# Fourier mixing and gated convolution FFN: a held load, earlier tables, unread products, and a one-row product in the first chunk

## Chip, cores, metric

One core of one Trainium2 chip. The metric is device time of one execution in microseconds (us), median over runs; the span that a trace shows is about 2 us shorter than the time of the same run. Engines: PE multiplies matrices (TensorE), DVE is VectorE, ACT is ScalarE, POOL is GpSimd, and SP's queue (SPq) issues most loads. The granted clock is the share of full speed at which PE was let run; half clock is 0.5.

## The reference, cut

```python
X = np.fft.fft(x, axis=1)                 # x: 8 x 3136 x 256
X = np.fft.fft(X, axis=2).real            # then the FFN on it:
h = np.maximum(X @ w_in, 0.0)             # 256 -> 1024
conv_out[s] = sum(conv_w[k] * h[s + k - 1] for k in range(3))
out = (h * sigmoid(conv_out)) @ w_out     # 1024 -> 256
```

The kernel folds x by the symmetries of the transform, multiplies it with tables along the sequence, and multiplies the transform over D into w_in beforehand (G). Steps run over (batch, chunk of the sequence, block f of 128 features): 8 x 4 x 8 = 256 steps. The feature D/2 has no partner under the symmetry. It adds to each step a product of a row over the sequence (`er`) and a column over the features (`ge`). Each half of a batch's x comes by one plain load and four gathers (indirect loads that POOL issues). The tables along the sequence are loaded in part, and ACT completes them by copies with either sign; I call that mirroring. The products with them come in odd units first, then even units.

## The kernel before: the parts concerned

```python
w_in[0].load(nc.sync); w_cv.load(nc.scalar)
nc.scalar.dma_start(out=dm, in_=dft_dim[:, :, 0:2])      # dm: table over D
for h in range(2):
    for f in load_ops(0, h, nc.sync, nc.scalar): f()     # x of batch 0, two halves
...
for g in range(2):                                       # sets the "written" bits of pa's two banks
    mm(psa.tile(...), dm[:, 0, g, :], dm.rearrange("p t g i -> p (t g i)"), True, True)
narrow_in(0); blocks(0)                                  # w_in from 64-bit words; G of quarter 0
ops = fold_ops(0)
for f in ops[0:4]: f()
nc.gpsimd.tensor_copy(tabs[1][0:1, 0, 0, 0:1], xh[0, 1][0:1, 0, 0, 0:1])   # releases the tables
for par in (1, 0): load_tables(par)
for i in (1, 2, 3): w_in[i].load(nc.sync)
for f in ops[4:]: f()
w_out.load(nc.sync)
# odd units (DFT), row(): er <- qt by DMA
narrow_in(1)                                             # DVE, while PE makes the even units
# feature, even units; after the feature: flip(), store(), spread(0, all chunks): er -> DRAM -> eb
...
def seed(s):                                             # ACT writes the D/2 part into pa
    act(pa[s][:, 0:n], eb[b, c], AF.Copy, scale=ge[:, f:f + 1])
def products(s):                                         # PE; pb: one product, pa: two or one
    mm(pb[s][:, 0:n], G[0:P-1, 1, fs], PQ[b][1][...], True, True)
    mm(pa[s][:, 0:n], G[:, 0, fs], PQ[b][0][...], False, not triple(s))
# cycle t: products(t+1), copies(t+1) [ACT], combine(t) [DVE], narrowings [DVE],
#          seed(t+2), first_tap(t) [ACT], other_taps(t-1) [DVE], gate(t-2) [DVE, POOL],
#          mm2(t-3) [PE], blocks [PE]
# narrow(2) in cycles 0, 1; narrow(3) in 2, 3; w_out's eight parts in 1 to 8; blocks(1) before cycle 0
```

A narrowing turns a half quarter of w_in (or an eighth of w_out) from 64-bit words into fp32: seven DVE operations, 2.58 us. `blocks(i)` multiplies quarter i with dm into G and `ge`. I call the DVE operation that joins pa and pb of step t combine(t); combine(0) is the first DVE operation of the steps.

Of the kernel before, what the change touches and what calls it, by code (L numbers as in the profile page):

```python
# [9 lines left out]
F32 = mybir.dt.float32  # L10
I32 = mybir.dt.int32
U32 = mybir.dt.uint32
AF = mybir.ActivationFunctionType
# [23 lines left out]
def kernel(  # L37
# [10 lines left out]
    nc = tc.nc  # L48
    B, S, D = x.shape
    F = moe_w_in.shape[1]  # L50
    P = 128
# [16 lines left out]
    xp = ctx.enter_context(tc.tile_pool(name="xp", bufs=2))  # L68
# [11 lines left out]
    psa = ctx.enter_context(tc.tile_pool(name="psa", bufs=2, space=PSUM))  # L80
    psb = ctx.enter_context(tc.tile_pool(name="psb", bufs=1, space=PSUM))
# [6 lines left out]
    act = nc.scalar.activation  # L88

    def mm(o, l, r, start, stop):  # L90
        nc.tensor.matmul(o, l, r, start=start, stop=stop, skip_group_check=True)  # L91

    def spare():

        return pso.tile([P, 2, D], F32, name="po", tag="po").rearrange("p a d -> p (a d)")
# [4 lines left out]
    xh, wt, ea = {}, {}, {}  # L100
# [4 lines left out]
    nc.gpsimd.memset(sg[:, 0], -1.0)  # L105
    nc.gpsimd.memset(sg[:, 1], 1.0)

    def load_ops(b, h, eng, other=None):


        def plain():
            t = xp.tile([P, 8, 2, D], F32, name="xh", tag="xh")
            xh[b, h] = t
            eng.dma_start(out=t[0:NP, 0:4], in_=bass.AP(
                tensor=x.tensor, offset=x.offset + (b * S + 1 + 2 * h) * D,
                ap=[[HQ * D, NP], [Q4 * D, 4], [1, 2 * D]]))

        def zero():
            t = xh[b, h]
            for s0, n, r in ((0, 4, 0), (4, 3, 1), (7, 1, 0)):  # L120
                (other or eng).dma_start(out=t[NP:KR, s0:s0 + n], in_=bass.AP(
                    tensor=x.tensor, offset=x.offset + (b * S + r * Q4) * D,
                    ap=[[D, 1], [Q4 * D, n], [0, 2], [1, D]]))

        def mirrored(m):
            def f():
                nc.gpsimd.indirect_dma_start(  # L127
                    out=xh[b, h][0:NP, 7 - m].rearrange("p q d -> p (q d)"),
                    out_offset=None,
                    in_=bass.AP(tensor=x.tensor, offset=x.offset,  # L130
                                ap=[[2 * D, B * S // 2], [1, 2 * D]]),
                    in_offset=bass.IndirectOffsetOnAxis(ap=idx[0:NP, 0:1], axis=0),
                    element_offset=(b * S + (4 - m) * Q4 - HO + 2 * (1 - h)) * D)
            return f
        return [plain] + [zero] * h + [mirrored(m) for m in range(4)]
# [59 lines left out]
    tabs = [const.tile([P, n, HQ, HE], F32, name="tab%d" % n) for n in (2, 4)]  # L195
    PQ, eb, er = {}, {}, {}
# [5 lines left out]
    def load_tables(par):  # L202


        st = slice(2 * par, 2 * par + 2)
        to = tabs[par][:, 0:2].rearrange("p s q i -> p s (q i)")
        n = HQ * HE
        m = NP // 2 // 16 * 16
        for i in range(2):
            nc.sync.dma_start(out=to[i:2 * m:2], in_=dft_seq[0:m, st, HQ * i:HQ * (i + 1)]  # L210
                              .rearrange("p s q i -> p s (q i)"))
        assert NP == 2 * m + 2
        nc.sync.dma_start(out=to[2 * m:NP], in_=bass.AP(
            tensor=dft_seq.tensor, offset=dft_seq.offset + (m * 4 + 2 * par) * NQ * HE,
            ap=[[n, 2], [NQ * HE, 2], [1, n]]))
        nc.sync.dma_start(out=to[NP:KR], in_=bass.AP(
            tensor=dft_seq.tensor, offset=dft_seq.offset + ((NP * 4 + 2 * par) * NQ - HQ + 2) * HE,
            ap=[[n, 1], [NQ * HE, 2], [1, n]]))
# [141 lines left out]
    def spread(b, cs):  # L360

        for c in cs:
            ch = chunks[c]
            eb[b, c] = ebp.tile([P, HN], F32, name="eb", tag="eb")[:, 0:ch.k1 - ch.k0]
            nc.sync.dma_start(out=eb[b, c], in_=ed[b:b + 1, ch.k0:ch.k1].to_broadcast([P, ch.k1 - ch.k0]))
# [31 lines left out]
    chunks = [Chunk(c) for c in range(len(CUTS))]  # L397
    HW = max(c.w for c in chunks)
    HN = max(c.k1 - c.k0 for c in chunks)
    left = const.tile([P, NF, P], F32, name="left")  # L400
# [52 lines left out]
    dm = gp.tile([P, 2, 2, P], F32, name="dm", tag="g")  # L453
    N4 = F // 4
# [3 lines left out]
    def raw_in(i):  # L458
        def f(sh):
# [5 lines left out]
    w_in = [Weight(w4[i], moe_w_in[:, i * N4:(i + 1) * N4].rearrange("(t p) n -> p t n", p=P), raw_in(i))  # L465
            for i in range(4)]
    w_in[0].load(nc.sync)
    w_cv.load(nc.scalar)
    nc.scalar.dma_start(out=dm, in_=dft_dim[:, :, 0:2])
    for h in range(2):  # L470
        for f in load_ops(0, h, nc.sync, nc.scalar):
            f()
    wout = const.tile([P, NF, D], F32, name="wout")
    G = const.tile([P, 2, F], F32, name="G")
    ge = const.tile([P, NF], F32, name="ge")
    cw = const.tile([P, 3, NF], F32, name="cw")

    def blocks(i):


        w = w4[i]
        for g in range(2):
            p = spare()
            for t in range(2):
                mm(p[:, 0:N4], dm[:, t, g, :], w[:, t], t == 0, t == 1)
            nc.scalar.copy(out=G[:, g, i * N4:(i + 1) * N4], in_=p[:, 0:N4])
        p = spare()
        for m in range(NF // 4):
            for t in range(2):
                mm(p[:, m:m + 1], w[:, t, m * P:(m + 1) * P], dm[:, t, 1, P - 1:P], t == 0, t == 1)  # L490
        nc.scalar.copy(out=ge[:, i * NF // 4:(i + 1) * NF // 4], in_=p[:, 0:NF // 4])

    def taps():
        p = spare()
        mm(p[:, 0:3 * NF], cw24[:, 0], ident, True, True)
        nc.scalar.copy(out=cw.rearrange("p k m -> p (k m)"), in_=p[:, 0:3 * NF])
# [2 lines left out]
    rows = out.rearrange("b s d -> (b s) d")  # L499
    hs, gs, pa, pb, po, nb = {}, {}, {}, {}, {}, {}  # L500

    def cut(s):
        b, c, f = s
        ch = chunks[c]
        return ch, ch.k1 - ch.k0, slice(f * P, (f + 1) * P)

    def seed(s):

        b, c, f = s
        ch, n, fs = cut(s)  # L510
        pa[s] = psa.tile([P, 512], F32, name="pa", tag="pa")
        act(pa[s][:, 0:n], eb[b, c], AF.Copy, scale=ge[:, f:f + 1])  # L512

    def triple(s):

        return s[0] == 0 and s[1] * NF + s[2] < TRIPLE
# [7 lines left out]
    def products(s):  # L524
        b, c, f = s
        ch, n, fs = cut(s)
        pb[s] = psb.tile([P, 512], F32, name="pb", tag="pb")
        mm(pb[s][:, 0:n], G[0:P - 1, 1, fs], PQ[b][1][0:P - 1, ch.k0:ch.k1], True, True)
        mm(pa[s][:, 0:n], G[:, 0, fs], PQ[b][0][:, ch.k0:ch.k1], False, not triple(s))
        if triple(s):  # L530
            mm(pa[s][:, 0:n], G[0:P - 1, 1, fs], PQ[b][1][0:P - 1, ch.k0:ch.k1], False, True)

# [80 lines left out]
    def narrow_in(i):  # L613
        for t in range(2):
            w_in[i].narrow(t, slice(0, N4))

    w_cv.narrow(0, slice(0, P))
    taps()

    for g in range(2):  # L620
        mm(psa.tile([P, 512], F32, name="pa", tag="pa"), dm[:, 0, g, :], dm.rearrange("p t g i -> p (t g i)"),
           True, True)
    narrow_in(0)
    blocks(0)
    ops = fold_ops(0)
    for f in ops[0:4]:
        f()

    nc.gpsimd.tensor_copy(tabs[1][0:1, 0, 0, 0:1], xh[0, 1][0:1, 0, 0, 0:1])
    for par in (1, 0):  # L630
        load_tables(par)
    for i in (1, 2, 3):
        w_in[i].load(nc.sync)
    for f in ops[4:]:
        f()
    w_out = Weight(wout, moe_w_out.rearrange("(c p) o -> p c o", p=P),
                   lambda sh: xp.tile(sh, I32, name="raw", tag="xh"))
    w_out.load(nc.sync)
    begin, us, row, flip, store = units(0)
    begin()  # L640

# [8 lines left out]
    for i, u in enumerate(odds):  # L650
# [2 lines left out]
        u.fin()  # L653
        if i == 1:
            row()
    narrow_in(1)
    mend_row(0, half)
    for i, u in enumerate(us[j] for j in (4, 2, 3, 7, 8)):
        u.matmuls(0, 1)
        u.copy()  # L660
        u.fin()
        if i == 0:
            flip()
            store()
            spread(0, range(len(chunks)))
            for f in load_ops(1, 0, nc.sync):
                f()

    steps = [(b, c, f) for b in range(B) for c in range(len(chunks)) for f in range(NF)]
    per = len(chunks) * NF  # L670
    side = {}

    def at(cycle, where, fn):
        side.setdefault((cycle, where), []).append(fn)

    for i in (2, 3):
        for t in range(2):
            at(2 * i - 4 + t, "dve", lambda i=i, t=t: w_in[i].narrow(t, slice(0, N4)))
        at(2 * i - 3, "pe", lambda i=i: blocks(i))
    for c in range(NF):  # L680
        at(1 + c, "dve", lambda c=c: w_out.narrow(c, slice(0, D)))
    for j, fn in enumerate(load_ops(1, 1, nc.sync)):
# [10 lines left out]
    for b in range(1, B):  # L693
        ops = fold_ops(b)
        c0, n = fold_at[b]
# [10 lines left out]
        c0, n = dft_at[b]  # L706
# [18 lines left out]
    n = len(steps)  # L725
# [1 line left out]
    seed(steps[1])  # L727
    products(steps[0])
    copies(steps[0])
    blocks(1)  # L730
    for t in range(n + LAG):
        def run(where):
            for fn in side.get((t, where), []):
# [88 lines left out]
```

## Time and profile before

| | kernel before |
|---|---|
| time, median of 3 runs | 1265.25 us (1264.12 to 1265.77) |
| span of the profiled execution | 1265.2 us |
| PE / DVE / ACT / POOL busy | 94 / 91 / 70 / 31 % |
| tables issued / first mirrored by ACT | 20.80 / 30.24 us |
| combine(0) / combine(5) | 58.79 / 95.72 us |

A timeline line reads: start, duration, engine, line of the kernel, operation, out<-in, shapes, count, and in brackets the engine's idle time before it with what ended it. A window line reads: window, its length, busy us of PE, PE weight load, DVE, ACT, POOL (with counts), granted PE clock as a share of full, DMA share, GB/s.

### The profile page before, as it was taken

The page shows a single profiled execution, that of the slowest core. Times are in us where ns is not written, and L with a number is a line of the kernel's source. Part 1 is how long each engine was busy: PE and PEld are TensorE (multiplying, and loading weights), DVE is VectorE, ACT ScalarE, POOL GpSimd, SP SyncE. Part 2 cuts the span into 40 slices and gives each one's busy share as a digit, 9 for nine tenths or more (in the row PEclk, how much of TensorE's full clock was granted, in tenths as well). Part 3 has the DMA queues.
Part 4 walks back from the last instruction along what each step waited for, and adds up shares of the span by engine and source line. Part 5 has one row for each costly group of instructions (what it writes and reads, how often), then busy time and mean ns, then how long its engine had stood idle before and what let it go on. Part 6 is the DMA issues. An engine that isn't in the chain of part 4 may idle for free.

```text
span 1265.2 us, 15611 instructions
## 1 busy us (share of the span) xinstructions
PE 1190.4 (94%) x4898; PEld 896.7 (71%) x4898; DVE 1148.7 (91%) x1753; ACT 886.5 (70%) x1847; POOL 396.3 (31%) x501
## 2 busy tenths in 40 slices
PE   2877999899999999999999999999999999999998
PEld 1545677677677767677677777777777777777776
DVE  7499999999999989899899988998999878899996
ACT  1354666677767767777767777776777778788885
POOL 4202642424333234242423324242322213222222
PEclk8799999999999999999999999999999999999999
DMA  7601321212212003020202103120011001010000
GB/s 196 204 1 32 96 77 45 58 34 69 68 53 69 29 19 93 25 84 25 73 23 64 49 26 90 31 84 1 26 45 33 30 26 39 27 28 30 30 25 31
DMA packets 47762, 66.06 MB, mean 52 GB/s; under 512 B 5756, under 2 KB 35348, under 8 KB 47680
## 3 DMA queue, kind: packets, MB, share of 16 engines
q1 hardware_dynamic: 42227, 51.91, 13.4%
q0 software_dynamic: 5120, 12.85, 3.6%
q8 instruction: 39, 0.64, 0.2%
q10 hardware_dynamic: 333, 0.30, 0.1%
q14 instruction: 43, 0.35, 0.1%
HBM read 39.26 MB, written 25.74 MB: 51 GB/s over the span
## 4 chain that ended last, share of the span: by engine, by line
PE 62%; DVE 23%; issue 6%; ACT 4%; DMA 3%; POOL 1%; SPq 0%; DVEq 0%; POOLq 0%; ACTq 0%
PE po L91 38%; PE pb L91 9%; PE pa L91 8%; DVE g L567 7%; PE pd L91 6%; DVE h L555 3%; DVE g L588 3%; ACT nb L544 2%; DVE xh L152 1%; DVE xh L163 1%; DVE w L179 1%; ACT g L580 1%; DMA eb<-ed 1%; DMA er<-qt 1%; DVE w L180 1%
## 5 line engine op out<-in xcount | busy, mean ns | idle before, releaser
L91 PE MATMUL po<-wout,g 128*128 128x256 f32 x3072 | 715.1, 382 | 37.2 <-DVE g L588 33.2
L91 PEld LDWEIGHTS po<-wout,g 128*128 128x128 f32 x3072 | 578.6, 190 | 198.9 <-DVE g L588 76.6
L567 DVE SCALAR_TENSOR_TENSOR g<-h,cw,g 128x770 f32<-128x770 f32 (+1 forms) x512 | 554.0, 1082 | 10.6 <-ACT g L561 1.5
L587 POOL TENSOR_TENSOR g<-g,h 128x385 f32<-128x385 f32 (+1 forms) x256 | 238.5, 932 | 738.7 <-ACT g L580 525.2
L580 ACT ACTIVATE g<-g 128x385 f32<-128x385 f32 (+2 forms) x512 | 244.4, 528 | 224.5 <-DVE g L567 224.2
L544 ACT ACTIVATE nb<-pb 128x386 f32<-128x386 f32 (+2 forms) x484 | 213.3, 494 | 83.8 <-PE pb L91 82.9
L555 DVE CUSTOM_DVE_ANT_0 h<-pa,nb 128x386 f32<-128x386 f32 (+2 forms) x498 | 258.2, 558 | 9.9 <-ACT h L541 9.1
L561 ACT ACTIVATE g<-h,cw 128x770 f32<-128x770 f32 (+1 forms) x256 | 243.6, 951 | 0.2 <-DVE h L555 0.2
L91 PE MATMUL pb<-qt,G 127*128 127x387 f32 (+2 forms) x512 | 215.2, 501 | 3.5 <-DVE qt L277 1.8
L91 PE MATMUL pa<-pt,G 128*128 128x387 f32 (+2 forms) x512 | 212.9, 496 | 3.3 <-ACT pa L512 3.3
L512 ACT ACTIVATE pa<-eb,ge 128x387 f32<-128x387 f32 (+2 forms) x256 | 154.0, 602 | 5.2 <-DMA eb<-ed 5.2
L588 DVE TENSOR_TENSOR g<-g,h 128x385 f32<-128x385 f32 (+1 forms) x256 | 151.7, 593 | 1.3 <-ACT g L580 1.3
L91 PEld LDWEIGHTS pa<-pt,G 128*128 128x128 f32 x512 | 96.8, 190 | 78.4 <-issue 19.0
L91 PE MATMUL pd<-tab,w 98*128 98x196 f32 (+3 forms) x448 | 117.4, 374 | 0.0
L91 PEld LDWEIGHTS pb<-qt,G 127*128 127x128 f32 x512 | 94.3, 191 | 26.1 <-issue 5.6
L127 POOL DMA_INDIRECT xh<-in_x_dram,idx x64 | 96.6, 1509 | 18.1 <-issue 12.9
L91 PEld LDWEIGHTS pd<-tab,w 98*128 98x128 f32 (+1 forms) x448 | 82.9, 190 | 12.8
L607 ACT COPY os<-po 128x256 f32<-128x256 f32 x196 | 58.0, 396 | 10.3 <-PE po L91 5.9
L152 DVE TENSOR_TENSOR xh<-xh 98x1020 f32<-98x1020 f32 (+1 forms) x32 | 45.3, 1419 | 3.6 <-DMA xh<-in_x_dram,idx 3.6
L163 DVE TENSOR_TENSOR xh<-xh 98x1024 f32<-98x1024 f32 (+1 forms) x32 | 40.5, 1266 | 0.1
L181 POOL COPY w<-xh 98x4 f32<-98x4 f32 (+1 forms) x32 | 24.5, 765 | 19.6 <-DVE xh L163 14.5
L339 POOL TENSOR_TENSOR er<-as 1x197 f32<-1x197 f32 (+1 forms) x16 | 13.0, 812 | 55.8 <-ACT as L331 29.3
(94 smaller groups left out, 406.3 us busy)
## 6 DMA issues: line engine op xcount, KB each, us to landing
out_dram<-os SPq DMA_DIRECT2D x192, 128.0 KB
xh<-in_x_dram SPq DMA_DIRECT2D x16, 784.0 KB
eb<-ed SPq DMA_DIRECT2D x16, 193.5 KB
tab<-dft_seq_dram SPq DMA_DIRECT2D x4, 589.5 KB
raw<-in_moe_w_in_dram SPq DMA_DIRECT2D x4, 512.0 KB
raw<-in_moe_w_out_dram SPq DMA_DIRECT2D x1, 2048.0 KB
eb<-ed SPq DMA_DIRECT2D x8, 209.0 KB
eb<-ed SPq DMA_DIRECT2D x8, 193.0 KB
```

The source lines that it names most:

```text
L91: nc.tensor.matmul(o, l, r, start=start, stop=stop, skip_group_check=True)
L127: nc.gpsimd.indirect_dma_start(out=xh[b, h][0:NP, 7 - m].rearrange("p q d -> p (q d)"), out_offset=None, in_=bass.AP(tensor=x.tensor, offs ...
L152: vt(a[:, :, :, 1:D], a[:, :, :, 1:D], r[:, :, :, D - 1:0:-1], op=ALU.add)
L512: act(pa[s][:, 0:n], eb[b, c], AF.Copy, scale=ge[:, f:f + 1])
L544: act(nb[s][:, i, cols], p[:, cols], AF.Copy, scale=-1.0 if i else 1.0)
L555: nc.vector._custom_dve(TENSOR_ADD_SAT, out=to, in0=a[:, cols], in1=c[:, i, cols], s0=BIG, s1=0.0)
L561: act(gs[s], hs[s][:, 0:n], AF.Copy, scale=cw[:, 0, s[2]:s[2] + 1])
L567: stt(out=g, in0=h[:, k:k + n], scalar=cw[:, k, f:f + 1], in1=g, op0=ALU.mult, op1=ALU.add)
L580: act(gs[s][:, c], gs[s][:, c], AF.Sigmoid)
L587: gt(g[:, p], g[:, p], h[:, p], op=ALU.mult)
L588: vt(g[:, v], g[:, v], h[:, v], op=ALU.mult)
L607: nc.scalar.copy(out=osb[:, j % 2], in_=pt[:, j % 2])
```

## The change

The intent is a shorter head. The second half of x is held until the gathers of the first half are issued. The tables no longer wait behind fold work in POOL's order. PE makes products that nobody reads while it waits. The D/2 part of the first chunk comes from a one-row product in place of a trip through DRAM. Without seeds in the first chunk, `ge` of quarter 1 is no longer needed at once, and its narrowing moves from the head into cycle 0.

```diff
-    nc.scalar.dma_start(out=dm, in_=dft_dim[:, :, 0:2])
     for h in range(2):
-        for f in load_ops(0, h, nc.sync, nc.scalar):
+        for f in load_ops(0, h, nc.sync, nc.scalar, h == 1):   # held: POOL memset ahead of the load
             f()
+        if h == 1:
+            nc.sync.dma_start(out=dm, in_=dft_dim[:, :, 0:2])
+    nc.gpsimd.tensor_copy(tabs[1][0:1, 0, 0, 0:1], xh[0, 1][0:1, 0, 0, 0:1])
+    for par in (1, 0):
+        load_tables(par)
+    ... w_in[1..3].load                      (both from behind the fold; w_out.load goes behind row())
 ... blocks(i):
+        for t in range(2):
+            mm(p[0:1, N4:2 * N4], dm[:, t, 1, P - 1:P], w[:, t], t == 0, t == 1)
+        nc.scalar.copy(out=left[0:1, 2 * i:2 * i + 2]..., in_=p[0:1, N4:2 * N4])
 ... seed(s):
+        if not first(s):                     # first: batch 0, chunk 0
+            if s in ((0, 1, 0), (0, 1, 1)):
+                start_all(pa[s], wout[:, 0, 0:P], wout[:, 0:2]...)
             act(pa[s][:, 0:n], eb[b, c], AF.Copy, scale=ge[:, f:f + 1])
 ... products(s):
-        mm(pa[s][:, 0:n], G[:, 0, fs], ..., False, not triple(s))
+        mm(pa[s][:, 0:n], G[:, 0, fs], ..., first(s), not triple(s))
+        if first(s):
+            mm(pa[s][:, 0:n], left[0:1, f, :], er[b][:, ch.k0:ch.k1], False, False)
 ...
-    for g in range(2): mm(psa.tile(...), ...)    # the two products for the "written" bits go
     narrow_in(0)
+    keep_on(2)                               # keep_on(n): n unread products of 512 columns
     blocks(0)
+    keep_on(4)
 ...
-    narrow_in(1)
-            spread(0, range(len(chunks)))
+            spread(0, range(1, len(chunks)))
+    keep_on(2)
-    for i in (2, 3):
+    for i in (1, 2, 3):
         for t in range(2):
-            at(2 * i - 4 + t, "dve", ... w_in[i].narrow(t, slice(0, N4)))
-        at(2 * i - 3, "pe", lambda i=i: blocks(i))
+            at((0, 1, 3)[i - 1] + (i > 1) * t, "dve", ... w_in[i].narrow(t, slice(0, N4)))
+        at(2 * i - 2, "pe", lambda i=i: blocks(i))
-    blocks(1)
```

## The prediction

> **What bounds the kernel now.** I read the page's slices first, then short windows of the first 130 us, then the timeline of that stretch, then the chain of waits. The slices say where to look: PE and DVE are both nine tenths busy from the fifth slice to the end, and only the first four slices (126 us) are thin. The change touches nothing after step 9 of 256, so the question is how much earlier the steady part begins and what work has been pushed into it.
>
> Windows of the kernel before (busy us of each engine, granted PE clock, DMA share, GB/s):
>
> ```profile
> 19.00:20.00 1.00, 0.33 (x3) 0.24 (x3) 1.00 (x3) 0.16 (x1) 1.00 (x3) 1.00 0.00 0
> 20.00:21.00 1.00, 0.00 (x0) 0.00 (x0) 0.97 (x2) 0.00 (x0) 0.78 (x1) 1.00 0.00 0
> ...
> 24.00:25.00 1.00, 0.00 (x0) 0.00 (x0) 1.00 (x2) 0.00 (x0) 0.00 (x0) 0.50 1.06 258
> ...
> 35.00:36.00 1.00, 1.00 (x4) 0.68 (x3) 0.00 (x0) 0.21 (x1) 0.00 (x0) 0.50 1.00 268
> ```
>
> The loads of x end at 18.2 us, nothing moves until 22.2, and then the tables move at 240 to 260 GB/s. PE stops at 19.3 us, is at half clock from 23.4, and gets full clock back at 36.6 only. Timeline of the kernel before (start, us, engine, line, what, and the idle time before it with its releaser):
>
> ```profile
> 15.72 1.22 DVE L152 TENSOR_TENSOR xh<-xh 98x1020 f32<-98x1020 f32 x1 [1.95 <-DMA xh<-in_x_dram,idx]
> ...
> 19.60 1.18 POOL L629 COPY tab<-xh 1x1 f32<-1x1 f32 x1
> ...
> 20.80 1.38 SPq L210 DMA_DIRECT2D tab<-dft_seq_dram  x2
> ...
> 29.97 0.99 PE L91 MATMUL po<-tab,w 98*128 98x196 f32 x2 [10.64 <-DMA tab<-dft_seq_dram]
> ...
> 54.59 1.09 ACT L512 ACTIVATE pa<-eb,ge 128x386 f32<-128x386 f32 x2 [5.18 <-DMA eb<-ed]
> ...
> 58.79 0.56 DVE L555 CUSTOM_DVE_ANT_0 h<-pa,nb 128x385 f32<-128x385 f32 x1 [6.35 <-ACT h L541]
> ```
>
> The first half of x is complete at 15.7 us only, because the second half shares the bandwidth. POOL's one-element copy, which releases the tables, stands behind fold work in POOL's order, so the tables are issued at 20.8 and land at 29.97. Later, the seed of step 0 waits for the D/2 feature to go out and come back spread over all partitions. The chain of waits has the two round trips:
>
> ```profile
> 41.57 4.68 DMA er<-qt
> ...
> 48.85 1.31 DMA ed<-er
> 50.17 4.39 DMA eb<-ed
> ```
>
> From step 1 on DVE is the bound: these windows are 10 us each.
>
> ```profile
> 90.00:100.00 10.00, 10.00 (x40) 7.30 (x40) 9.55 (x20) 5.83 (x12) 1.83 (x3) 1.00 0.01 2
> 100.00:110.00 10.00, 5.53 (x21) 3.42 (x19) 9.72 (x17) 3.15 (x7) 0.97 (x2) 1.00 0.00 1
> 110.00:120.00 10.00, 7.24 (x27) 5.36 (x28) 9.62 (x19) 5.84 (x12) 2.86 (x5) 0.94 0.00 0
> ```
>
> So the head has three serial waits (tables, cold PE, the feature's spread), and behind it a DVE queue with no slack until about 175 us. **A gain in the head counts only until combine(0), the first DVE operation of the steps, at 58.79; after that DVE work counts one for one.**
>
> **What the Trainium skill says.** "TensorE: Matmul & The Clock Gate", section "Part 1: The HAM clock gate": PE falls to half clock after an idle window of about 3.4 us and needs about as long a busy one to come back. The trace agrees: idle from 19.33, half from about 23.4; busy from 32.20, full from about 36.6 (4.4 us). "DMA: Bandwidth & Descriptors", section "Issuing engines are not separate DMA queues": transfers from all issuers interleave on the same engines. The trace agrees: the first half of x lands at 15.7 though it was issued first. "PSUM — Partial Sum Buffer", section "The four PSUM rules": writes of ACT do not touch the bits that decide between adding and overwriting, and a starting matmul clears them for the whole bank. Hence the unread starting products before steps 8 and 9, whose ACT seeds follow starting matmuls of 386 columns and are themselves 387 wide; no time in this trace bears on it.
>
> **The change, part by part.** Times below are estimates from durations in the trace before.
>
> 1. Second half of x held behind a POOL memset after the first half's four gathers. These are issued until 7.04, so the held load goes out near 7.5, when 1.4 MB of the first 2.1 MB have moved; there is no hole in the DMA. The first half is complete near 10.5 instead of 15.7, and DVE, free of narrowing at 10.86, folds it without stalls: 9.4 us of work, done near 20.3 instead of 23.4. The whole fold ends near 29.3 instead of 32.1. This is not on the path by itself, as the tables are later than what needs it.
>
> 2. Tables released sooner. The copy waits for the held plain load (784 KB, sharing about 260 GB/s with gathers: near 15.5) and for 1.18 us of its own, so the tables go out near 16.5. The rest of x ends at 18.2 as before, since the bytes are the same. The 4 us hole in the DMA closes: the first tables took 29.97 - 22.2 = 7.8 us of moving, so they land near 25.7. **Gain 4.3 us.**
>
> 3. Unread products. The dim table now stands behind the held load and lands near 16.5 (before: 13.3). Two products of 512 columns cold (1.7 us each by 3.48 us for two), blocks(0) with its new row products (2.8 + 0.9), four products warm (3.4): PE is busy until 26 or 27 and so enters the table products warm. Those begin in earnest when ACT has mirrored (2.2 us after landing, 27.9): 7 pairs in 3.9 us, then 4.5 for the second halves, 0.9 for the feature: 37.2, which is 11.5 after landing instead of 43.16 - 29.97 = 13.2. **Gain 1.7 us.** The even units follow, 5.9 us as before, to 43.1.
>
> 4. Feature by a one-row product. The spread of chunk 0 and its seed (5.18 us of wait) go. A one-row product costs what its 386 columns cost, 0.82 us for the pair of instructions, like its neighbours. The row's round trip stays, but the 2 MB of w_out are now issued after it, so it should take near the 2.1 us that the six later waits for it average ((17.5 - 4.7)/6) and land before the even units end. narrow(1) has left this place too, so the last DVE work follows the copies at once. After 43.1: two unread products 1.7, four pairs 3.3, the ReLU 0.5, latencies 0.3: combine(0) near 48.9. Before, it took 58.79 - 49.0 = 9.8 us; now 5.8. **Gain 4.0 us.**
>
> Sum until combine(0): 10.0 us.
>
> 5. narrow(1) moved into cycle 0. Two halves of 2.58 us (43.34 to 45.92 for one) leave a place where DVE had slack and enter the stretch where it has none: **cost 5.2 us**. Against it, DVE's idle 2.8 us before combine(1) (61.9 to 64.70, caused by blocks(1) standing in front of products(1)) goes: **gain 2.8**. Net cost 2.4.
>
> 6. Beside other work: eight row products (6.6 us), two starting products (1.7), row products in the later blocks (2.8): about 11 us of PE in a stretch where PE is little over half busy. Eight seeds of 0.59 us leave ACT, four copies come. No share in the sum. One exception: blocks(1) now waits for the end of narrow(1), and products(2) behind it finish close to the time when DVE wants combine(2); with a PE that cooled in that wait this is late by up to 2 us. I book 0.7.
>
> Total 10.0 - 2.4 - 0.7 = 6.9 us; 1265.25 - 6.9 = 1258.3, said as 1258. Everything after cycle 5 is ordered by cycles and should shift as it is.
>
> **Rivals.** (a) *The head's gain is eaten by the queue behind it.* For: DVE's windows above, and narrow(1) moves into them. If blocks(1) to blocks(3), each now waiting on a narrow in its own cycle, stall DVE each time, 3 to 5 us more go and the time is 1262 or 1263. Against: except around combine(2), products are emitted a cycle (8 us) ahead. (b) *The unread products hold up PE.* For: the dim table is later, and PE takes its orders in turn, so four products that end after the tables land push the odd units. That would cost 1 to 2 us: 1260. Against: ACT's mirroring leaves 2.2 us of room. (c) *The tables are bound by their transfer, not by the release.* If the remaining x shares the bandwidth with them in full, they land near 28 and 2.3 us of the gain go: 1260 to 1261. Against: the idle DMA from 18.2 to 22.2 is real. (d) *More than I count*: the tables land at 24 and blocks(1) stays warm; then the sum nears 10 us, 1255. (e) A gain of over 2% would need 25 us; the whole span before combine(0) is 58.8, of which the loads alone need half. A loss of 2% has no candidate short of a stall of every step.
>
> **Range and chances.** The total rests on three gains of about 4, 2 and 4 us and a cost of about 3, each uncertain by 1 to 2 us; taken as independent that is some 3 us, and 8 in 10 lie within about 5: 1253 to 1263. A side of 2% lies five such errors away on the fast side and further on the slow one: 0.01 each.
>
> **What would show it.** Right: tables issued near 16.5 and the first table product near 26; no half clock between 27 and 50; no wait for eb in chunk 0; combine(0) near 49; combine(5), at 95.72 before, near 88 to 89, and the end shifted by the same. Wrong: combine(0) near 49 but combine(5) after 92 would mean that the steps' DVE queue took the gain (a); a first odd product well after the landing of its table, with PE in unread products, would mean (b); tables landing after 28 would mean (c). If combine(5) has shifted by 7 and the end has not, then the steady part does not shift as a whole, which I have assumed and not shown.

## More of the kernel before

The profiled execution of the kernel before took 1267.16 us, more than all of its timed runs.

## The result

The changed kernel took 1263.92 us median (1263.78 to 1265.42, 4 runs), the kernel before 1264.68 us in the same rounds: ratio 0.9996, 95% interval 0.9979 to 1.0013, the same. Ratios here are the mean time of one kernel's fast runs over that of the other's of the same rounds, so not quite the ratio of the medians quoted. A repeat with five more rounds gave 0.9994 (0.9981 to 1.0007). The result lies 0.9 us above the range's upper end.

Timeline of the kernel after, the lines that answer to those shown of before:

```profile
17.46 0.19 POOL L478 COPY tab<-xh 1x1 f32<-1x1 f32 x1 [4.67 <-DMA xh<-in_x_dram]
17.68 1.32 SPq L213 DMA_DIRECT2D tab<-dft_seq_dram  x2
18.92 3.78 PE L91 MATMUL pb<-dm 128*128 128x512 f32 x4 [13.04 <-DMA dm<-dft_dim_dram]
27.27 3.68 PE L91 MATMUL pb<-dm 128*128 128x512 f32 x8
27.44 0.16 ACT L504 COPY ge<-po 128x2 f32<-128x2 f32 x1 [1.14 <-PE po L91]
27.60 1.91 ACT L233 ACTIVATE tab<-tab 99x392 f32<-99x392 f32 x4
30.78 8.10 PE L91 MATMUL po<-tab,w 98*128 98x196 f32 x32
...
51.18 0.56 DVE L581 CUSTOM_DVE_ANT_0 h<-pa,nb 128x385 f32<-128x385 f32 x1 [4.34 <-ACT h L567]
...
56.79 0.55 DVE L581 CUSTOM_DVE_ANT_0 h<-pa,nb 128x385 f32<-128x385 f32 x1
56.93 3.95 PE L91 MATMUL po<-win,dm 128*128 128x256 f32 x10 [1.87 <-DVE win L422]
66.09 0.56 DVE L581 CUSTOM_DVE_ANT_0 h<-pa,nb 128x385 f32<-128x385 f32 x1 [1.62 <-ACT h L567]
```

POOL's release now waits for the held load itself, which lands at 17.4 us. The dim table behind it lets PE begin at 18.92. The four unread products start 0.3 us before ACT mirrors the tables and keep PE until 30.8.

The mirroring itself did not wait for the tables here. ACT's line of the kernel before, and the load in the kernel after's chain of waits, show the difference:

```profile
30.24 1.90 ACT L230 ACTIVATE tab<-tab 99x392 f32<-99x392 f32 x4 [10.72 <-DMA tab<-dft_seq_dram]
...
7.60 11.28 DMA dm<-dft_dim_dram
```

Before, ACT sat idle until the tables landed. After, it mirrors directly behind its copy of `ge`, which waited for PE's blocks(0), which waited for the dim table. The landing records in the trace file (no view of the profile prints them) put the last piece of the tables at 26.53 us, 27.10 in the repeat, against 30.13 and 29.70 in the two traces of before. So about 1 us of the earlier landing was lost in ACT's order.

combine(0) is at 51.18 instead of 58.79. Then cycle 0 carries two narrowings (51.65 to 56.79), blocks(1) starts after them, and DVE waits 1.62 us for step 2, a wait that the kernel before does not have (its wait of 2.79 us before combine(1) is gone in exchange).

Windows of the kernel after around that wait:

```profile
55.00:57.00 2.00, 0.13 (x2) 0.07 (x1) 1.86 (x6) 0.00 (x0) 0.00 (x0) 1.00 0.55 151
57.00:59.00 2.00, 2.00 (x6) 1.19 (x6) 1.85 (x6) 0.37 (x1) 0.00 (x0) 0.69 0.02 6
59.00:61.00 2.00, 1.88 (x5) 0.34 (x4) 1.84 (x6) 0.46 (x2) 0.00 (x0) 0.50 0.00 0
```

PE waits for the narrowings, loses its clock at 57.8, and makes blocks(1) at half clock. DVE, which the narrowings now load, had idled in the head. Three DVE lines of the same timeline show it:

```profile
35.97 0.36 DVE L299 TENSOR_TENSOR as<-as,po 128x196 f32<-128x196 f32 x1 [7.70 <-ACT as L295]
...
42.44 0.51 DVE L280 TENSOR_TENSOR qt<-as,po 128x197 f32<-128x197 f32 x1 [2.48 <-ACT as L276]
...
51.18 0.56 DVE L581 CUSTOM_DVE_ANT_0 h<-pa,nb 128x385 f32<-128x385 f32 x1 [4.34 <-ACT h L567]
```

That is 14.5 us of empty DVE ahead of combine(0), and 5.2 us of work that would fit into it standing behind.

### The profile page after: what moved, and what is told of

The parts are those of the page before. It is cut to its first block, busy times and chain, and to the rows that moved or that the text cites. A ratio compares the mean times of both kernels' runs of the same rounds, so it can differ in the third digit from the quotient of the medians.

```text
span 1261.8 us, 15700 instructions
## 1 busy us (share of the span) xinstructions
PE 1203.2 (95%) x4946; PEld 898.4 (71%) x4946; DVE 1148.8 (91%) x1753; ACT 884.7 (70%) x1843; POOL 396.4 (31%) x502
## 4 chain that ended last, share of the span: by engine, by line
PE 68%; DVE 19%; issue 5%; ACT 4%; DMA 2%; POOL 2%; SPq 0%; POOLq 0%; ACTq 0%; DVEq 0%
PE po L91 42%; PE pb L91 10%; PE pa L91 9%; PE pd L91 7%; DVE g L593 6%; DVE g L614 3%; DVE h L581 3%; ACT nb L570 2%; DVE xh L166 1%; DMA dm<-dft_dim_dram 1%; DVE xh L155 1%; ACT g L606 1%; POOL xh L130 1%; DVE w L182 1%; DVE w L183 1%
## 5 line engine op out<-in xcount | busy, mean ns | idle before, releaser
L536 ACT ACTIVATE pa<-eb,ge 128x387 f32<-128x387 f32 (+2 forms) x248 | 149.3, 602 | 0.7 <-PE pa L91 0.7
L91 PEld LDWEIGHTS pa<-pt,G 128*128 128x128 f32 x512 | 96.9, 189 | 73.7 <-issue 18.9
L280 DVE TENSOR_TENSOR qt<-as,pd 128x197 f32<-128x197 f32 (+1 forms) x14 | 7.3, 519 | 24.9 <-ACT as L276 24.9
```

What stands on the lines that cost most here:

```text
L91: nc.tensor.matmul(o, l, r, start=start, stop=stop, skip_group_check=True)
```

## The experiments

**Theory Q.** The change shortens the head, but a DVE queue without slack stands behind combine(0). The change puts 5.2 us of narrowing into that queue, and a PE that cooled while waiting for it adds a stall; together they take back most of the gain. **Rival S.** The steady part levels out any early shift, so nothing done in the head reaches the end. **Rival P.** The unread products delay useful ones and are the loss.

Each kernel ran beside the kernel before on one chip in the same rounds.

### Repeats: before_again, after_again (no edit)

> The unchanged kernel before, for a second trace. Theory V (the first trace of before was a slow one, since its span of 1265.2 us lies 1.4 to 3.2 us above those of four timed runs): a new trace has its first DVE step operation combine(0) at 55 to 57.5 instead of 58.79, PE's half-clock stretches before 62 us being shorter, and a span of 1262 to 1263.5. Rival (the head is the same in all runs and the spread lies later): combine(0) at 58.8 within 0.3 again, and any difference in span arises after 200 us.

> The unchanged kernel after, for a second trace and five more rounds. Theory V: PE is at full clock until 57 us, so combine(0) repeats at 51.2 within 0.3; the blocks of cycle 0 fall into a half-clock stretch or not, so combine(2) moves between 65 and 66.5. Ratio to before 0.998 to 1.000.

before_again: 1265.57 us, ratio 1.0 (0.9987 to 1.0013); after_again: 1264.3 us, ratio 0.9994. Timeline of before_again:

```profile
57.47 0.56 DVE L555 CUSTOM_DVE_ANT_0 h<-pa,nb 128x385 f32<-128x385 f32 x1 [4.23 <-ACT h L541]
63.04 0.56 DVE L555 CUSTOM_DVE_ANT_0 h<-pa,nb 128x385 f32<-128x385 f32 x1 [2.45 <-ACT h L541]
```

combine(0) came at 57.47, as expected for a first trace that was slow (58.79), and the span was 1263.4 us. So 1.3 us of the wait from which I worked out the gain, and 1.8 us of the span, were not there in another run. In the clock records the half-clock stretch around the first products was 50.5 to 60.8 us in one trace and 51.9 to 58.8 in the other. The repeat of after had combine(0) at 51.59 (expected 51.2 within 0.3), the blocks of cycle 0 in a half-clock stretch of 55.0 to 61.8, and combine(2) at 67.24 (expected 65 to 66.5: the stall, 2.4 us over the 7.6 us that combine(1) to combine(2) takes without it, was larger still).

From combine(5) to the end the four traces need 1169.5, 1169.4, 1169.7 and 1170.2 us. The steady part shifts as a whole within 0.8 us, which speaks against S.

### a_narrow_head: narrow(1) back in the head

```diff
+    narrow_in(1)                 # after row(), where the kernel before has it
     mend_row(0, half)
-    (narrow(1) in cycle 0, narrow(2) in 1, 2, narrow(3) in 3, 4; blocks in 0, 2, 4)
+    (narrow(2) in cycles 0, 1, narrow(3) in 2, 3; blocks in 0, 1, 3)
```

> The changed kernel with the narrowing of the second quarter of w_in back in the head, and the other quarters in cycles 0 to 3 as before. Theory Q (the DVE queue behind the head has no slack, so the moved 5.2 us and the stall of 1.62 us at combine(2) took the gain): combine(0) 0.5 to 1.5 us later than 51.18, combine(5) at 86 to 88 instead of 92.14, end 4 to 6 us earlier than the kernel after. Rival S (the steady part levels out any early shift): combine(5) earlier but the end within 1 us of the kernel after.

1258.7 us, ratio 0.9945 (0.9932 to 0.9958): 5.6 us less than after_again by the medians. Timeline, combine(0), (1), (2) and (5):

```profile
52.67 0.56 DVE L581 CUSTOM_DVE_ANT_0 h<-pa,nb 128x385 f32<-128x385 f32 x1 [2.92 <-ACT h L567]
55.71 0.55 DVE L581 CUSTOM_DVE_ANT_0 h<-pa,nb 128x385 f32<-128x385 f32 x1
63.32 0.55 DVE L581 CUSTOM_DVE_ANT_0 h<-pa,nb 128x385 f32<-128x385 f32 x1
...
86.84 0.55 DVE L581 CUSTOM_DVE_ANT_0 h<-pa,nb 128x385 f32<-128x385 f32 x1
```

combine(0) is 1.1 us later than in after_again, for the narrowing stands before the last DVE work of the head. combine(5) is 6.5 us earlier, and the end with it. There is no wait before combine(2). Q holds in size and place; S is out.

### a_less_unread: without the last six unread products

```diff
     blocks(0)
-    keep_on(4)
 ...
-    keep_on(2)
     steps = [...]
```

> The changed kernel without its four unread products after the first blocks and without the two before the steps (the first two stay). Theory P (unread products stand in front of useful ones): the first odd products begin at 29.5 to 29.7 instead of 30.78, the first pa product at 45.6 to 46.2 instead of 48.05, combine(0) near 49 instead of 51.18, end 2 us earlier. Rival C (they are what keeps the clock up): PE falls to half clock between 27 and 35 us or after 45, and combine(0) is at 51 or later.

1268.16 us, ratio 1.0017 (1.0004 to 1.0029): slower by 0.2%, with one of six runs at 1263.19. The trace is of a run of 1268.17. Windows:

```profile
28.00:31.00 3.00, 1.33 (x7) 0.89 (x7) 0.33 (x1) 2.88 (x7) 1.78 (x2) 1.00 0.97 238
31.00:34.00 3.00, 3.00 (x9) 2.23 (x8) 0.00 (x0) 2.14 (x5) 0.00 (x0) 0.57 1.05 306
...
58.00:61.00 3.00, 3.00 (x7) 0.78 (x6) 2.73 (x9) 0.37 (x1) 0.00 (x0) 0.50 0.01 3
...
64.00:67.00 3.00, 3.00 (x6) 1.17 (x4) 0.00 (x0) 0.49 (x1) 0.00 (x0) 0.50 0.00 0
```

The first odd product came earlier (27.92), and still the odd units ended later, at half clock from 31.4 to 34.8. combine(0), at 50.59, was 0.6 to 1.0 us earlier, not 2. Then PE was at half clock from 55.3 to 72.4, and DVE waited 6.07 us before combine(2). Rival C is right here and P is wrong as an account of the loss: the unread products cost up to 1.3 us of order (30.8 against 29.5, when mirroring ends), and without them the clock costs more in the traced run. Four more runs lie within 0.6 us of it; the sixth, at 1263.19, was faster than every run of the kernel after and has no trace.

### b_row_only and b_hold_only: one part of the change alone

```diff
 b_row_only:  the kernel before
+    one-row products and start_all, spread(0, range(1, ...))
 b_hold_only: the kernel before
+    held second half of x; release and loads of tables and w_in ahead of the fold
```

> The kernel before with only the one-row product for the D/2 feature (and the two starting products that it needs). Theory A (the wait for the spread is only one of three things that hold combine(0); behind it stand the late last DVE work and a PE at half clock): the wait for eb is gone, the first pa product moves from 54-55 us to 52 to 52.7, but with the added product at half clock combine(0) is at 56.5 to 58 (before: 57.5 and 58.8 in two traces); end within 1.5 us of before. The prediction's step 4 alone (a gain of the order of 4 us from the removed wait): combine(0) at 53 to 55, end 3 to 5 us earlier.

> The kernel before with only the held second half of x and the earlier release of the tables. Theory A: tables issued at 17.5 to 18 instead of 20.8, landed at 27.5 to 28.3 instead of 29.5 to 30, PE cold as before, everything behind 2 us earlier: combine(0) at 55.5 to 56.8, end 1.5 to 2.5 us earlier. Rival S (later waits level it out): combine(0) as before, end within 0.7 us.

b_row_only: 1265.51 us, ratio 1.001 (0.9991 to 1.003). Timeline:

```profile
52.24 1.55 PE L91 MATMUL pa<-pt,G 128*128 128x386 f32 x2
53.72 1.06 PE L91 MATMUL pa<-er,left 1*128 1x386 f32 x2
...
56.25 0.56 DVE L571 CUSTOM_DVE_ANT_0 h<-pa,nb 128x385 f32<-128x385 f32 x1 [3.81 <-ACT h L557]
...
63.53 0.56 DVE L571 CUSTOM_DVE_ANT_0 h<-pa,nb 128x385 f32<-128x385 f32 x1 [4.15 <-ACT h L557]
```

The wait for the spread is gone, and pa starts at 52.24 as expected. combine(0) gains 1.2 us on the faster trace of before, which combine(1) gives back at once: 63.53 against 63.04, since PE has more to make before it. One of the four runs took 1270.2 us; the others do not differ from before. **By itself the one-row product brought no measured gain.**

b_hold_only: 1264.35 us, ratio 0.9989 (0.9974 to 1.0005), not clear of zero and short of the 1.5 to 2.5 us expected. Its release was at 19.46 us, not 17.5 to 18. The dim table is loaded at the start here, so the held load shares with one transfer more; it landed 2 us later. First mirroring at 28.71 (before: 30.24 and 29.81), combine(0) at 56.71.

### a_dm_early: the dim table loaded at the start, as before

```diff
+    nc.scalar.dma_start(out=dm, in_=dft_dim[:, :, 0:2])    # right after w_cv.load
-        if h == 1:
-            nc.sync.dma_start(out=dm, in_=dft_dim[:, :, 0:2])
```

> The changed kernel with the dim table loaded from ACT's queue at the start, as before. Theory P (the unread products stand in front of the odd units since the dim table is late): PE's first product at 13.3 to 14 instead of 18.9, unread products over by 26, odd units begin when ACT has mirrored, 29.5 to 30, instead of 30.8 to 31.2; combine(0) 1.0 to 1.5 us earlier than 51.2-51.6 and the end as much. Rival C (PE then idles before the tables and cools): a half-clock stretch between 27 and 36 us, and combine(0) not earlier.

1266.34 us, ratio 1.0018 (1.0001 to 1.0035), with one of four runs at 1270.46; without that run the difference is within the noise. The unread products were over at 22.6, PE then idled for 5.17 us and was at half clock from 28.0 to 34.8. The release slipped to 19.05. combine(0): 52.59. Rival C again: the early dim table cost 1.0 to 1.4 us at combine(0), although the late one had looked like a flaw to me.

### a_warm0: unread products in cycle 0

```diff
+    at(0, "pe", three unread products into a spare bank)
     at(0, "pe", blocks(1))
```

> The changed kernel with three unread products in cycle 0, ahead of the blocks of quarter 1 that wait there for the narrowing. Theory W (the stall of DVE at combine(2), 1.6 and 2.4 us in two traces, is these blocks at half clock): no half-clock stretch between 53 and 63 us, combine(1) to combine(2) 7.6 to 7.8 us instead of 9.3 and 10.0, everything behind 1.6 to 2.4 us earlier, end 1.5 to 2.5 us earlier than the kernel after. Rival (the blocks are late at full clock too, since they start after the narrowing): combine(1) to combine(2) over 8.8 us at full clock.

1263.79 us, ratio 0.9988 (0.9974 to 1.0001). Timeline, combine(2):

```profile
64.98 0.56 DVE L581 CUSTOM_DVE_ANT_0 h<-pa,nb 128x385 f32<-128x385 f32 x1 [0.20 <-ACT h L567]
```

Full clock from 53 to 63 us, and combine(1) to combine(2) takes 7.88 us instead of 9.30 and 10.04. So W is right: the stall was blocks(1) at half clock. combine(5) was at 91.00 (92.14 and 93.29). But PE fell to half clock later (82.0 to 85.4 and 92.2 to 102.5 in the clock records), DVE waited 0.40 and 0.49 us before combine(6) and combine(7), and the span of this trace, 1262.1 us, lies between those of the two traces of after. The gain at combine(2) is shown; the 1.5 to 2.5 us that I expected at the end did not come.

### b_row_narrow: one-row product and moved narrowing, without the other parts

```diff
 b_row_only
-    narrow_in(1)                 # out of the head
+    (narrow and blocks of quarters 1 to 3 in the cycles of the kernel after)
```

> The kernel before with the one-row product and, beside it, narrow(1) and its blocks moved into the steps as in the kernel after; loads, tables and unread products as before. Theory Q (a narrowing in the head costs the last DVE work of the head about 1 to 3 us, one in the queue costs 5.2 us plus a stall): combine(0) at 52.5 to 54.5 (56.25 with the row product alone), combine(2) to combine(5) as in the kernel after, combine(5) at 93.5 to 96.5 against 94.56; the end within 1.5 us of that of the row product alone. Rival (moving it is the gain of the change): combine(5) at 92 or earlier.

1266.66 us, ratio 1.0026 (1.0012 to 1.004), with two of five runs at 1270. combine(0) came at 53.50, 2.75 us earlier than with the row product alone, and combine(5) at 95.22, 0.66 later than its 94.56. DVE waited 2.41 us before combine(2). The move gives in the head and takes more in the queue, as Q says. Moving the narrowing without the row product could not be tried: the seed of step 2, emitted in cycle 0, would read `ge` before it is written.

### a_best, a_best2, a_best3: the narrowings spread over the idle DVE of the head

```diff
 all three: narrow(1) and part or all of narrow(2) ahead of combine(0)
 a_best:   narrow(1): one half before, one after the odd units; narrow(2) before combine(0);
           narrow(3) in cycles 0, 1; dim table early, keep_on(8) in place of keep_on(4)
 a_best2:  the same, but the dim table late as in the change, keep_on(2) in place of keep_on(4)
 a_best3:  as a_best2, narrow(1) after the odd units and before combine(0), half of narrow(2) with
           it; the rest of narrow(2) in cycle 0, narrow(3) in 1, 2
```

> The changed kernel with the dim table early, eight unread products in place of four, narrow(1) in two places of the head where DVE idles (before the odd units' last work and after it), narrow(2) ahead of combine(0), narrow(3) in cycles 0 and 1. Theory Q: 10.3 us of DVE work leave the queue behind combine(0) and the stall at combine(2) goes; combine(0) at 50.5 to 52.5, combine(5) at 80 to 83.5 (after: 92 to 93; with narrow(1) in the head: 86.8), the end 9 to 12 us earlier than the kernel after, ratio to before 0.990 to 0.993. Rival: PE's products, not DVE, set the pace of cycles 1 to 4 by then, and combine(5) is at 85 or later.

> The version with 10.3 us of narrowing out of the queue, but with the dim table behind x as in the changed kernel, and two unread products after the first blocks instead of four. Theory: tables issued at 17.6 to 18 (19.6 with the dim table early), odd units from 29.5 to 30.2 at full clock, combine(0) at 52 to 53.5, combine(5) at 81.5 to 83.5 (84.49 with the dim table early), end 1 to 3 us earlier than that version, ratio to before 0.989 to 0.992. Rival C: two unread products are too few, PE cools, and nothing is gained over that version.

> As a_best2, but narrow(1) stands after the odd units and before combine(0), one half each, with half of narrow(2); the rest of narrow(2) and narrow(3) in cycles 0 to 2: the odd units' last DVE work no longer waits for the load of w_in. Theory: the odd units' last DVE work starts at 34.5 to 35 instead of after 36.5, combine(0) at 51 to 52.5, but one half more (2.6 us) in the queue: combine(5) at 82 to 84, end within 1 us of a_best2. Rival: the later work of the head decides, combine(0) as in a_best2 and the end 2.6 us later than a_best2.

| | time, us | ratio to before | combine(0) | combine(5) | span |
|---|---|---|---|---|---|
| a_best | 1255.86 | 0.992 (0.9907 to 0.9934) | 54.25 | 84.49 | 1254.0 |
| a_best2 | 1252.52 | 0.9902 (0.9887 to 0.9917) | 51.97 | 80.72 | 1250.0 |
| a_best3 | 1253.54 | 0.9908 (0.9893 to 0.9923) | 50.86 | 84.02 | 1253.6 |

In a_best the early dim table brought the cold odd units again (half clock from 29.5 to 36.4), so combine(0) and combine(5) missed their ranges by 1.7 and 1.0 us. Timeline of a_best2:

```profile
26.60 1.96 PE L91 MATMUL pb<-dm 128*128 128x512 f32 x4
28.40 8.39 PE L91 MATMUL po<-tab,w 98*128 98x196 f32 x32
34.31 0.29 DVE L415 TENSOR_SCALAR win<-raw 128x256 int32<-128x256 int32 x1 [5.99 <-DMA raw<-in_moe_w_in_dram]
...
51.97 0.55 DVE L581 CUSTOM_DVE_ANT_0 h<-pa,nb 128x385 f32<-128x385 f32 x1
```

Two unread products end about when the tables are usable, the odd units run warm from 28.40, 2.4 us sooner than in the kernel after (no run isolates the two products fewer), and DVE narrows as soon as w_in lands. DVE goes from its narrowings straight into combine(0); of its idle time in the head, the 5.99 us before w_in lands are the largest piece left. All three are correct. **a_best2 beats both kernels by about 12 us.** a_best3 had the earliest combine(0) of the three and still ended 1 us after a_best2: its trace has one half narrowing more behind combine(0). That trace is of its slowest run (1255.61 us); the timed gap of 1.0 us is less than the 2.6 us that its rival had, and the intervals overlap.

## Why the prediction was wrong

The first two columns are my sums of gain so far, against the slow trace that I read and as measured by the means of two traces of each kernel (us). Of the 6.2 us missing at the end, 1.2 went in step 2, 1.3 in step 3, 0.8 in step 4 and 1.5 in the stall of steps 5 and 6; about 1.4 stays unexplained.

| until | predicted | measured | from |
|---|---|---|---|
| last landing of the tables | 4.3 | 3.1 | 29.92 to 26.82 |
| first mirroring of the tables | 4.3 | 2.2 | 30.03 to 27.81 |
| end of the feature product | 6.0 | 3.5 | 43.41 to 39.91 |
| combine(0) | 10.0 | 6.7 | 58.13 to 51.39 |
| combine(5) | 6.9 | 2.1 | 94.84 to 92.72 |
| end of the span | 6.9 | 1.7 | 1264.3 to 1262.65 |
| timed medians | 6.9 | 0.8 and 0.7 | two sets of rounds |

- **Step 1** held in its own terms: the first half of x was complete in time and DVE folded without a stall, ending at 28.3 (I had 29.3).
- **Step 2 failed by 1.2 us.** I let the held load land "near 15.5" and the tables go out "near 16.5". It landed at 17.4 (17.1 in the repeat), while gathers that share the DMA engines with it were still landing (the last at 19.0), and the tables went out at 17.7. They landed 3.1 us earlier than before, not 4.3. Rival (c) would have shown in a landing after 28, which did not come: the release was late, not the transfer behind it.
- **Step 3 failed by 1.3 us.** From the landing of the tables to the end of the feature product it gained 0.4 us, not 1.7. The dim table was later than I said (18.9, not 16.5), and with it blocks(0). ACT mirrored only behind the copies of blocks(0), 1.1 and 0.9 us after the landing (in a_dm_early, with blocks(0) done early, 0.1 us after it, 28.11 and 28.22), and the unread products then held the tables' products for another 1.3 us. I had taken ACT's mirroring as 2.2 us of room and not seen that it stands behind PE's work itself. So rival (b) was real, by its own sign: the first odd product came at 30.78, over 4 us after the landing. But a_less_unread and a_dm_early show that a PE left idle there cools and loses more.
- **Step 4** was right to 0.8 us in its place in the sum (3.2 against 4.0). The missing part is in the trace: before_again spent 1.8 us less than the first trace between the feature and combine(0). b_row_only shows that the gain is not the row product's own (1.2 us at combine(0)), and b_row_narrow that moving narrow(1) out of the head gave 2.75 us more, which the queue took back. A one-row product took 0.91 us, not 0.82.
- **Step 5 and the exception in step 6 failed together.** I put the narrowing at a net 2.4 and the stall at 0.7, 3.1 in all; combine(0) to combine(5) became 4.6 us longer (36.71 to 41.33). The move itself was as I sized it. The mis-sized term is the stall: 1.6 and 2.4 us, because blocks(1) ran at half clock, which I had named and given a third. a_warm0 shows the cause, a_narrow_head that both go with the narrowing's place. Step 6 also called PE "little over half busy" there; the three windows that it rests on average 7.6 of 10 us.
- **The steady part** shifts nearly whole, as I assumed; 0.5 us of the mean difference after combine(5) stays unexplained. So does the further 1.0 us between traces and timed medians, which is no more than single runs of either kernel differ by.

Rival (a), "the head's gain is eaten by the queue behind it", came in part. I had named 3 to 5 us more than the 3.1 in the sum, from a stall at each of blocks(1) to blocks(3); 1.5 us more came, from blocks(1) alone. The larger lapse is in the form of the answer: errors that all cut the gain (a slow trace as the base, a late held load and dim table, a larger stall) were taken as independent, and the range of 1253 to 1263 was too tight at the top.

## What to carry to other kernels

Before work is moved out of a head, list the idle time of each engine on both sides of the place. Here 14.5 us of empty DVE stood before combine(0) and next to none behind it, and filling that time gave 12 us where the change as made gave none. Where PE would cool in a wait, unread products can keep it warm, but they should end when the wait ends. Take two traces of the base before a few microseconds are counted from one.

## What the Trainium skill lacked or had wrong

- "TensorE: Matmul & The Clock Gate", "Part 1: The HAM clock gate": the window of about 3.4 us is borne out. Half-clock stretches lasted 3.4 us (57.8 to 61.2), 6.8 (55.0 to 61.8), 10.2 (92.2 to 102.5) and 17.1 (55.3 to 72.4), multiples of it. But it says that full clock returns after one or more busy windows. In a_less_unread PE was recorded busy throughout 62.1 to 72.4, three such windows (ends of matmuls are modelled), and got full clock back only at 72.4; its pairs of products took 1.49 to 1.66 us there, against 0.81 to 0.92 at full clock. In a_warm0 it was recorded busy for all of 92.2 to 102.5. What counts as a busy window this section does not say.
- The same section speaks of idle windows. In the kernel after, PE was busy for 1.52 of the 3.41 us before the drop at 57.8, and its longest idle stretch was 1.87 us. In the repeat it was busy for 2.60 of the 3.42 us before the drop at 55.0, with no idle stretch over 0.82 us. Windows far from idle were enough.
- "DMA: Bandwidth & Descriptors", "Issuing engines are not separate DMA queues": interleaving is borne out, but the section has no figure for what this does to a load that is ordered late. The held load, released near 7.2 us, landed at 17.4; with 256 KB more on another queue it landed at 19.4 and 19.0.
- No page has a time for an fp32 product with a single row of weights. Its two instructions took 0.91 us for 386 columns, where its neighbours with 127 or 128 rows took 0.81 to 0.92.
- "PSUM — Partial Sum Buffer", "The four PSUM rules": all runs with the two starting products were correct; no run here leaves them out.
